# First loads in the order of need, the first Q and K by four blocks of x, and products of zeros in the first gaps

## The chip, the core and the metric

The kernel runs on one core of one Trainium2 chip. The metric is the device time of one execution in microseconds, and lower is better. The program is recorded in full before it runs: a planner written in Python inside the kernel decides the order of every instruction on every engine, and the chip then executes that fixed order, each engine in sequence, held back only by semaphores.

## The reference

Two attention layers with 32 heads of 32 columns over 2048 positions of 1024 columns each. Both share the shape of the projections; only the set of keys differs.

```python
qkv = (x @ wqkv).reshape(B, S, 3, H, Dh)            # q, k, v
# A: each position sees itself and 7 positions at steps of 2 behind it
# B: each position sees the 256 positions up to itself
scores = einsum("bhqd,bhkd->bhqk", q, k) * Dh ** -0.5
scores = where(mask, scores, -1e9)
o = einsum("bhqk,bhkd->bhqd", softmax(scores), v)
out = o.transpose(0, 2, 1, 3).reshape(B, S, D) @ wo
# result: concatenate([A, B], axis=-1)
```

## The kernel before, in words

The work is cut into eight units of 512 positions. Units 0 to 3 are layer B (called dense), units 4 to 7 are layer A (windows). A unit has eight groups of four heads. For each group the kernel computes Q and K (128 columns of heads by 512 positions), the scores, the softmax, and the product with V; after the groups comes the product with wo.

Precision comes from splitting. Each float32 operand becomes a high part in fp32r and a low part, the difference. A product of two operands is three matmuls, in the order of `TERMS`: high by high, high by low, low by high, each 128x128 by 128x512. `parts` (L222) makes the split: a cast on ACT (L228) or on DVE (L231) gives the high part, a subtraction on DVE (L234) gives the low part. One contraction block of Q therefore needs three matmuls, and Q and K of one group need 2 x 8 x 3 = 48.

`Stream` is the list of weights and x blocks in the order of use. The first six items are x block pair 0, the weights of Q, x pair 1, the weights of K, x pair 2 and x pair 3; each is 128 rows of 1024 floats (512 KB). An x item holds two contraction blocks; a weight item holds all eight, four in each half. `load_to` (L161) issues the first loads on the ACT queue: items 0 and 1 as halves in turn, then items 2 to 5 whole. Item 2 goes into the third raw buffer, items 3 to 5 borrow the room of `pbuf`, which is not needed yet. Later loads go on the POOL queue, each when a raw buffer is free again. `split_to` (L187) records the splits: at first items 0 and 1 half by half, then the others as the products reach them.

The product items of all units stand in the list `gemm`; three more lists hold the two rounds of score products (`ones`, `twos`) and the small product `rows` (`aux`). The loop at the end takes, at each step, the item that the planner's `Clock` says can start first. In the first group the order of the products is written by hand (the line with `x[0] + q[:2] + x[1] ...`). Ahead of it stand ten products of zeros (`WARM`), which read the still unused tile `qst[1]` after a memset.

In a dense group the first round (`first`, matmul `s<-kst,qst`) gives scores whose row maximum and sum DVE and ACT take. `log_sum` then turns both into one number per row, kept as a high and a low part in `hl`. The matmul `s<-ident,hl` (`rows`) turns these numbers over, DVE spreads them into the lower rows of `qst`, and only then can the second round (`s<-qst,kst`) run. The planner lets `rows` start at `e2 + HL_LATE`, which is 0.8 us after it believes `hl` is done. All four kinds of score product share a ring of four PSUM banks, `rs`.

Of the kernel before, what the change touches and what calls it, by code (L numbers as in the profile page):

```python
# [7 lines left out]
F32 = mybir.dt.float32  # L8
F32R = mybir.dt.float32r
# [5 lines left out]
P = 128  # L15
NG = 8
NK = 8
S = 512
# [3 lines left out]
NRAW, NP, NO, NS = 3, 768, 10, 4  # L22
# [7 lines left out]
CHUNK, ASKED, LEFT, FETCHED = 256, 150, 290, 7.0  # L30
EXTRA, EACH = 246, 5.2
P_LATE = 1.5
HL_LATE = 0.8
VPARTS = ((0,4),(4,2),(6,2))
V_SLOTS = {0:0,5:1,7:2}
O_SLOTS = {2: (0, 1), 3: (2, 3), 4: (4, 5), 5: (6, 7)}
# [14 lines left out]
C1, C3, CG, CV = 0.108, 0.2, 0.231, 0.242  # L51
CW = 1.36
ORDER = (0, 1, 2, 3, 4, 5, 6, 7)
BANK_LATE = 0.0
EARLY, WARM = 1.0, 10
TERMS = ((0, 0), (0, 1), (1, 0))


class Clock:
# [6 lines left out]
    HOLD = dict(sp=0.63, act=0.35, pool=0.6)  # L66
    MOVE = dict(load=(2.12, 0.14), store=(0.64, 0.4), copy=(1.18, 0.56),
                halo_out=(0.4, 0.68), halo_in=(0.55, 0.6), halo_few=(0.28, 0.51),
                half=(1.0, 0.14), part=(0.33, 0.56))

    def __init__(self):
        self.free = dict(pe=0.0, act=0.0, dve=0.0, pool=0.0, sp=0.0)
# [73 lines left out]
class Stream:  # L146
# [13 lines left out]

    def load_to(self, n):  # L161
        while not self.loaded:
            self.raw = {i: (self.raws.tile([P, 1024], F32, tag="raw", name="raw"), []) for i in range(2)}
            for h in range(2):
                for i in range(2):
                    raw, t = self.raw[i]
                    ap = self.items[i][1]
                    self.nc.scalar.dma_start(raw[:, S * h:S * h + S], ap[:, h] if len(ap.shape) == 3 else ap[:, S * h:S * h + S])
                    t.append(self.ck.load("half", self.ck.now))
            self.loaded = 2  # L170
        self.wanted = max(self.wanted, n)
        while self.loaded < min(n, len(self.items)):
            gate = self.gates.get(self.loaded)
            if gate and not gate():
                return
            k = self.loaded - NRAW
            if self.loaded >= self.wide and (self.loaded - self.wide) % (2 * NRAW) < NRAW:
                raw = self.room()
            else:
                raw = self.more[k] if 0 <= k < len(self.more) else self.raws.tile([P, 1024], F32, tag="raw", name="raw")  # L180
            ap = self.items[self.loaded][1]
            early = k < len(self.more)
            (self.nc.scalar if early else self.nc.gpsimd).dma_start(raw if len(ap.shape) == 2 else raw.rearrange("p (a b) -> p a b", a=2), ap)  # L183
            self.raw[self.loaded] = raw, (self.ck.load if early else self.ck.fetch)("load", self.ck.now)
            self.loaded += 1

    def split_to(self, n):  # L187
        while not self.split:
            (rx, tx), (rw, tw) = self.raw.pop(0), self.raw.pop(1)
            self.tiles[0], self.ready[0], self.ready[1] = [], [], []  # L190
            w = self.tiles[1] = self.wpool.tile([P, 2, 1024], F32R, tag="w", name="w")
            for h in range(2):
                c = slice(h * S, h * S + S)
                self.tiles[0].append(self.xpool.tile([P, 2, S], F32R, tag="x", name="x"))
                self.ready[0].append(self.parts(self.tiles[0][h], rx[:, c], tx[h], True))
                self.ready[1].append(self.parts(w[:, :, c], rw[:, c], tw[h], True))
            self.split = 2
            for i in range(2):
                self.ck.defer(self.ready[i][1], lambda n=i + len(self.more) + NRAW + 1: self.load_to(n))
# [44 lines left out]
def kernel(ctx, tc, xs, wqk, wv, wo, outs, units):  # L244


    nc = tc.nc
# [20 lines left out]
    ck = Clock()  # L268
# [236 lines left out]
    def latest(*ts):  # L505
        return None if any(t is None for t in ts) else max(ts)
# [788 lines left out]
    def attention(u, s):  # L1295
# [43 lines left out]
        def log_sum():  # L1339
            ln = small.tile([P, 16], F32, tag="ln", name="ln")  # L1340
            nc.scalar.activation(ln, h["sm"], AF.Ln)
            e = ck.use("act", 0.13, ck.now) - 0.03

            def parts():
                nl = small.tile([P, 16], F32, tag="nl", name="nl")
                nc.vector.tensor_tensor(nl, h["nm"], ln, op=ALU.subtract)
                hl = small.tile([P, 2, 16], F32R, tag="hl", name="hl")
                nc.vector.tensor_copy(hl[:, 0, :], nl)
                nc.vector.tensor_tensor(hl[:, 1, :], nl, hl[:, 0, :].bitcast(F32), op=ALU.subtract)
                e2 = ck.use("dve", 0.52, e, port=True)  # L1350
                aux.append(Item(lambda: latest(rs.when(BANK_LATE), e2 + HL_LATE), lambda: rows(hl), 0.08))

            ck.defer(e, parts)

        def rows(hl):
            ps, bank = rs.take()
            mm(ps[0:32, 0:P], hl.rearrange("p a b -> p (a b)"), cst["ident"], start=True, stop=True)

            def spread():

                h["rows"] = []
                for j in range(4):
                    nc.vector.tensor_tensor(q[96:P, j, :].rearrange("p (b s) -> p b s", s=P),  # L1363
                                            ps[0:32, None, 0:P].to_broadcast([32, 4, P]),
                                            cst["pick"][0:32, 4 * j:4 * j + 4, None].to_broadcast([32, 4, P]), op=ALU.mult)
# [104 lines left out]
        return one, two  # L1470


    aux, ones, twos, gemm = [], [], [], []
    for u in range(U):
        for s in range(NG):
# [4 lines left out]
    for p in plan:  # L1480
        if p[0] == "qk":
            new = qk_items(p[1], p[2])
            if p == ("qk", 0, 0):
                q, k, x = new[:NK], new[NK:], x_items(0)
                new = x[0] + q[:2] + x[1] + q[2:4] + k[:2] + x[2] + q[4:6] + k[2:4] + x[3] + q[6:] + k[4:]
            if NG - 1 not in V_SLOTS and p[2] == NG - 1 and p[1] + 1 < U:
                for g, x in reversed(list(enumerate(x_items(p[1] + 1)))):
                    new[NK + 2 * g:NK + 2 * g] = x
            gemm += new
        elif p[0] == "v":  # L1490
            new = v_items(p[1], p[2])
            if V_SLOTS.get(NG - 1) == p[2] and p[1] + 1 < U:
                m = 2 * VPARTS[p[2]][1]
                for g, x in reversed(list(enumerate(x_items(p[1] + 1)))):
                    new[m * g + XAT:m * g + XAT] = x
            gemm += new
        elif p[0] == "o":
            gemm += o_items(p[1], p[2])
        elif p[0] == "p":
            gemm += product(p[1], p[2])  # L1500
        elif p[0] == "vp":
            new = value_product(p[2])
            if VP_AT.get((p[1], NG - 1)) == p[2:] and p[1] + 1 < U:
# [6 lines left out]
    if WARM:  # L1510
        idle = qst[1][:, 0, :]
        nc.vector.memset(idle.bitcast(F32), 0.0)
        ps, bank = rs.take()
        for i in range(WARM):
            mm(ps, idle[:, :P], idle, start=True, stop=True)
        ck.free["pe"] = 0.6 + 0.43 * WARM
        rs.give(bank, ck.now)
    pos = {"a": 0, "1": 0, "2": 0, "g": 0}
    seqs = {"a": aux, "2": twos, "1": ones, "g": gemm}
    while True:  # L1520
# [21 lines left out]
        t, name = best  # L1542
# [52 lines left out]
```

## Time and profile before

| what | us |
|---|---|
| median of 3 runs (1808.05, 1811.09, 1811.22) | 1811.09 |
| the profiled execution, its own time | 1810.36 |
| the profiled execution, span from first to last instruction | 1808.5 |
| TensorE (PE) busy within the span | 1779.4 |
| VectorE (DVE) busy | 1294.4 |
| ScalarE (ACT) busy | 935.2 |
| GpSimd (POOL) busy | 417.7 |

A group of instructions in the profile is named by line, engine, operation and "written<-read" tiles. Times in a timeline row are start and length; the brackets give the idle time of the engine just before and what ended it. All matmuls are recorded through one helper, L276, so they are told apart by tiles: `g<-x,w` is a product of Q, K or of wo, `s<-qst` alone (without `kst`) is a product of zeros. ACTq, POOLq and SPq are the issuing of DMAs on those engines.

### The profile page before, as it was taken

Reading aid. Unit: us, or ns where it says so; the run is one execution under the profiler, and the core shown is the slowest. Engines: PE = TensorE matmul, PEld = TensorE weight load, DVE = VectorE, ACT = ScalarE, POOL = GpSimd, SP = SyncE. Lnnn points to the kernel's source line nnn. Section 1 sums busy time; section 2 is a strip of 40 time slices with the busy share of each in tenths; the row PEclk is TensorE's granted clock in tenths of the full one; section 3 lists DMA queues with packets and bytes.
Section 4 is the critical chain, followed back from the end, with each engine's and each line's share of the span. In section 5 each row is a group of like instructions: output and inputs, shape, how many; then the busy total and the mean of one; then the engine's idle time right before and its main releaser. Section 6 shows DMA issues by size and latency. Waiting matters only on the chain. (4 is left out here: it accounts for less than half of the span.)

```text
span 1808.5 us, 38436 instructions
## 1 busy us (share of the span) xinstructions
PE 1779.4 (98%) x14490; PEld 1439.0 (80%) x14490; DVE 1294.4 (72%) x2879; ACT 935.2 (52%) x2319; POOL 417.7 (23%) x967
## 2 busy tenths in 40 slices
PE   9999999999999999999999999999999999999999
PEld 7787778888777888777788788878887777887887
DVE  6777877768767668866678476665666768678866
ACT  5566466555666565655654543434443435356442
POOL 2323322232333233232324400110011101001220
PEclk9999999999999999999999999999999999999999
DMA  8455665645655556555556266666576568858984
GB/s 241 120 146 126 183 165 146 163 141 140 184 140 150 159 135 165 152 146 141 142 133 182 63 207 180 203 207 192 172 214 200 180 191 275 259 178 283 333 291 148
DMA packets 154649, 324.57 MB, mean 179 GB/s; under 512 B 18016, under 2 KB 58976, under 8 KB 154464
## 3 DMA queue, kind: packets, MB, share of 16 engines
q0 software_dynamic: 45792, 166.74, 30.5%
q1 hardware_dynamic: 97728, 134.40, 26.5%
q10 hardware_dynamic: 10944, 20.98, 3.1%
q8 instruction: 115, 1.88, 0.4%
q14 instruction: 70, 0.57, 0.1%
HBM read 201.33 MB, written 53.48 MB: 141 GB/s over the span
## 5 line engine op out<-in xcount | busy, mean ns | idle before, releaser
L276 PE MATMUL g<-x,w 128*128 128x512 f32 x3744 | 928.5, 395 | 5.1 <-ACT x L228 2.0
L276 PEld LDWEIGHTS g<-x,w 128*128 128x128 f32 x3744 | 692.0, 189 | 145.2 <-issue 5.6
L234 DVE TENSOR_TENSOR w<-raw,w 128x512 fp32r<-128x512 f32 x510 | 334.6, 697 | 51.7 <-ACT w L228 45.6
L276 PE MATMUL g<-w,x 128*128 128x256 f32 (+1 forms) x1872 | 332.8, 327 | 0.9 <-DVE w L234 0.7
L1323 DVE CUSTOM_DVE_ANT_0 s<-s,mask_d 128x384 f32<-128x384 f32 (+2 forms) x512 | 262.1, 553 | 98.1 <-PE s L276 96.8
L1328 ACT ACTIVATE s<-s,nm 128x384 f32<-128x384 f32 (+2 forms) x512 | 274.8, 538 | 101.4 <-DVE nm L1323 99.3
L276 PEld LDWEIGHTS g<-w,x 128*128 128x128 f32 x1872 | 276.7, 190 | 28.1 <-DVE w L234 2.2
L1387 POOL TENSOR_SCALAR_AFFINE_SELECT pbuf<-pbuf 128x128 f32<-128x128 f32 (+1 forms) x619 | 226.0, 393 | 300.9 <-ACT pbuf L1408 299.5
L1408 ACT ACTIVATE pbuf<-s 128x384 f32<-128x384 f32 (+2 forms) x480 | 202.7, 505 | 88.6 <-PE s L276 87.1
L276 PE MATMUL g<-r,w 128*128 128x512 f32 x768 | 190.8, 394 | 1.5 <-DVE r L1287 0.8
L276 PEld LDWEIGHTS g<-r,w 128*128 128x128 f32 x768 | 141.9, 188 | 30.9 <-DVE r L1287 1.8
L183 POOL DMA_DIRECT2D raw<-wqk x126 | 68.0, 540 | 417.2 <-DVE w L234 267.4
L276 PEld LDWEIGHTS s<-qst,kst 128*128 128x128 f32 x704 | 112.2, 189 | 43.6 <-ACT s L1328 17.7
L276 PE MATMUL s<-kst,qst 96*128 96x384 f32 (+2 forms) x512 | 142.9, 343 | 3.7 <-ACT s L1328 1.1
L231 DVE CAST w<-raw 128x1024 fp32r<-128x1024 f32 x176 | 122.1, 694 | 27.2 <-PE g L276 26.8
L276 PE MATMUL s<-qst,kst 128*128 128x256 f32 (+2 forms) x704 | 136.6, 302 | 4.6 <-ACT s L1328 3.5
L228 ACT CAST w<-raw 128x1024 fp32r<-128x1024 f32 (+1 forms) x80 | 82.7, 1038 | 75.8 <-PE g L276 29.0
L276 PEld LDWEIGHTS s<-kst,qst 96*128 96x128 f32 x512 | 92.9, 189 | 29.4 <-issue 6.1
L1328 ACT ACTIVATION_READ_ACCUMULATOR s<-s,nm 128x1 f32 x512 | 105.9, 207 | 0.0
L1190 ACT COPY wide<-band 32x512 f32<-32x512 f32 x128 | 79.0, 617 | 46.4 <-DVE band L1181 44.6
L276 PE MATMUL o<-pbuf,vbuf 128*32 128x384 f32 (+2 forms) x1408 | 91.1, 389 | 0.0
L1363 DVE TENSOR_TENSOR qst<-s,pick 32x512 fp32r<-32x512 f32 x128 | 79.3, 676 | 12.8 <-PE s L276 12.0
(90 smaller groups left out, 1327.7 us busy)
## 6 DMA issues: line engine op xcount, KB each, us to landing
raw<-wqk POOLq DMA_DIRECT2D x126, 512.0 KB, 4.6
raw<-wv POOLq DMA_DIRECT2D x60, 512.0 KB, 5.2
qst<-nat SPq DMA_DIRECT2D x96, 256.0 KB, 4.2
kst<-nat SPq DMA_DIRECT2D x96, 256.0 KB, 5.6
raw<-wo POOLq DMA_DIRECT2D x44, 512.0 KB, 4.9
raw<-xs POOLq DMA_DIRECT2D x28, 512.0 KB, 4.9
outs<-ost ACTq DMA_DIRECT2D x38, 256.0 KB, 2.8
kst<-halo SPq DMA_DIRECT2D x72, 128.0 KB, 4.5
```

Of the source, the lines that this page charges most:

```text
L183: (self.nc.scalar if early else self.nc.gpsimd).dma_start(raw if len(ap.shape) == 2 else raw.rearrange("p (a b) -> p a b", a=2), ap)
L228: nc.scalar.copy(t[:, 0, :], raw)
L231: nc.vector.tensor_copy(t[:, 0, :], raw)
L234: nc.vector.tensor_tensor(t[:, 1, c:c + 512], raw[:, c:c + 512], t[:, 0, c:c + 512].bitcast(F32), op=ALU.subtract)
L276: nc.tensor.matmul(out, left, right, **k)
L1190: nc.scalar.copy(diag[r:r + 32, :, :, c:c + 32], turned[r:r + 32, :, :, 1, :])
L1323: nc.vector.tensor_tensor_reduce(ps[:, :n], ps[:, :n], mask[:, cut:full], scale=-1.0, scalar=BIG, op0=ALU.add, op1=ALU.min, accum_out=nm)
L1328: nc.scalar.activation(ps[:, :n], ps[:, :n], AF.Exp, bias=nm, scale=-1.0, accum_out=sm)
L1363: nc.vector.tensor_tensor(q[96:P, j, :].rearrange("p (b s) -> p b s", s=P), ps[0:32, None, 0:P].to_broadcast([32, 4, P]), cst["pick"][0:32 ...
L1387: nc.gpsimd.affine_select(w, w, pattern=[[0, m], [step, n]], compare_op=ALU.is_ge, fill=0.0, base=base, channel_multiplier=chan)
L1408: nc.scalar.activation(w, ps[:, :pack * n].rearrange("p (j n) -> p j n", j=pack), AF.Exp)
```

## The change

The constant `HL_LATE` is gone, so the planner lets `rows` start at `e2`. The model's cost of a half load goes from 1.0 to 0.8, and a new kind `first` costs 1.4. The first loads follow the table `FIRST` of (item, half): both halves of x pair 0 and the first half of Q's weights, then x pair 1 whole, the first half of K's weights, the second half of Q's, x pair 2, the second half of K's, x pair 3. All six items are loaded and split at once, in that order. Of the first group's products, Q's first four blocks come first, then K's first four; the rest goes by two blocks of Q and two of K for each of x pairs 2 and 3. Behind Q's blocks 0, 1, 2 and 3 stand 1, 9, 1 and 4 products of zeros (`FILL`), written to the bank of the ten that were there.

```diff
-HL_LATE = 0.8
+FIRST = ((0, 0), (1, 0), (0, 1), (2, None), (3, 0), (1, 1), (4, None), (3, 1), (5, None))
+FILL = ((1, 1), (2, 9), (3, 1), (4, 4))
...
-                half=(1.0, 0.14), part=(0.33, 0.56))
+                half=(0.8, 0.14), first=(1.4, 0.14), part=(0.33, 0.56))
...
+            for i, h in FIRST:
+                raw, t = self.raw[i]
+                ap = self.items[i][1]
+                if h is None:
+                    self.nc.scalar.dma_start(raw.rearrange("p (a b) -> p a b", a=2), ap)
+                    t[:] = [self.ck.load("first", self.ck.now)] * 2
+                else:
                     self.nc.scalar.dma_start(raw[:, S * h:S * h + S], ap[:, h] if len(ap.shape) == 3 else ap[:, S * h:S * h + S])
-                    t.append(self.ck.load("half", self.ck.now))
-            self.loaded = 2
+                    t[h] = self.ck.load("half", self.ck.now)
+            self.loaded = 6
...
+            for i, g in FIRST:
+                raw, t0 = self.raw[i]
+                for h in (0, 1) if g is None else (g,):
+                    c = slice(h * S, h * S + S)
+                    t = self.tiles[i][:, :, c] if self.items[i][0] == "w" else self.tiles[i][h]
+                    self.ready[i][h] = self.parts(t, raw[:, c], t0[h], True)
+            self.split = 6
...
-                aux.append(Item(lambda: latest(rs.when(BANK_LATE), e2 + HL_LATE), lambda: rows(hl), 0.08))
+                aux.append(Item(lambda: latest(rs.when(BANK_LATE), e2), lambda: rows(hl), 0.08))
...
+    idle = qst[1][:, 0, :]
+
+    def fill(at, n):
+
+        def run():
+            mm(ps, idle[:, :P], idle, start=True, stop=True)
+
+        def after(last):
+            if last:
+                rs.give(bank, ck.now + ck.SEM)
+
+        return [(lambda: 0.0, run, CG, lambda i=i: after(at == FILL[-1][0] and i == n - 1)) for i in range(n)]
...
-                new = x[0] + q[:2] + x[1] + q[2:4] + k[:2] + x[2] + q[4:6] + k[2:4] + x[3] + q[6:] + k[4:]
+                f = dict(FILL)
+                new = x[0] + sum([q[i:i + 1] + fill(i + 1, f.get(i + 1, 0)) for i in range(4)], [])
+                for i in (1, 2, 3):
+                    new[new.index(q[2 * i]) if i < 2 else len(new):0] = x[i]
+                    if i == 1:
+                        new += k[:4]
+                    else:
+                        new += q[2 * i:2 * i + 2] + k[2 * i:2 * i + 2]
```

The first place where the order moves is the start. On PE (`s<-qst` are products of zeros, `g<-x,w` those of Q and K) before, and then in the change:

```order
L276 MATMUL s<-qst_123 128x512 x10
L276 MATMUL g<-x,w 128x512 x90
L276 MATMUL s<-kst_124,qst_122 128x128 x4
L276 MATMUL g<-x,w 128x512 x6
L276 MATMUL s<-kst_124,qst_122 128x256 x2
```

```order
L288 MATMUL s<-qst_124 128x512 x10
L288 MATMUL g<-x,w 128x512 x3
L288 MATMUL s<-qst_124 128x512
L288 MATMUL g<-x,w 128x512 x3
L288 MATMUL s<-qst_124 128x512 x9
L288 MATMUL g<-x,w 128x512 x3
L288 MATMUL s<-qst_124 128x512
L288 MATMUL g<-x,w 128x512 x3
L288 MATMUL s<-qst_124 128x512 x4
L288 MATMUL g<-x,w 128x512 x84
```

Fifteen products of zeros now stand among the first twelve real ones, and the 84 that follow run on without another kind between them. On ACT, at the same place, the loads and the first casts (`pbuf` is the borrowed room) before, and then in the change:

```order
L168 DMA raw<-xs 128x512
L168 DMA raw<-wqk 128x512
L168 DMA raw<-xs 128x512
L168 DMA raw<-wqk 128x512
L183 DMA raw<-xs 128x1024
L183 DMA pbuf<-wqk 128x1024
L183 DMA pbuf<-xs 128x1024 x2
L228 CAST x<-raw 128x512
L228 CAST w<-raw 128x512
L228 CAST x<-raw 128x512
L228 CAST w<-raw 128x512
```

```order
L175 DMA raw<-xs 128x512
L175 DMA raw<-wqk 128x512
L175 DMA raw<-xs 128x512
L172 DMA raw<-xs 128x1024
L175 DMA pbuf<-wqk 128x512
L175 DMA raw<-wqk 128x512
L172 DMA pbuf<-xs 128x1024
L175 DMA pbuf<-wqk 128x512
L172 DMA pbuf<-xs 128x1024
L240 CAST w<-raw 128x512
L240 CAST x<-raw 128x512 x3
L240 CAST w<-pbuf 128x512
```

There is one load more, x pair 1 moves from the fifth place to the fourth, and the second half of Q's weights from the fourth to the sixth. The first cast of x has gone to DVE.

The second place is on PE, ahead of the `rows` product of the sixth group. Here before, and then in the change:

```order
L276 MATMUL s<-kst_125,qst_123 128x384
L276 MATMUL g<-x,w 128x512 x3
L276 MATMUL s<-kst_125,qst_123 128x384 x4
L276 MATMUL o<-pbuf,vbuf_127 32x384 x8
L276 MATMUL s<-qst_122,kst_124 128x256 x4
L276 MATMUL s<-qst_122,kst_124 128x128 x4
L276 MATMUL s<-kst_125,qst_123 128x384 x3
L276 MATMUL o<-pbuf,vbuf_127 32x256 x4
L276 MATMUL o<-pbuf,vbuf_127 32x128 x4
L276 MATMUL g<-x,w 128x512 x3
L276 MATMUL s<-ident,hl 32x128
```

```order
L288 MATMUL s<-kst_126,qst_124 128x384 x2
L288 MATMUL g<-x,w 128x512 x3
L288 MATMUL s<-kst_126,qst_124 128x384 x3
L288 MATMUL o<-pbuf,vbuf_128 32x384 x8
L288 MATMUL s<-qst_123,kst_125 128x256 x4
L288 MATMUL s<-qst_123,kst_125 128x128 x4
L288 MATMUL s<-kst_126,qst_124 128x384 x3
L288 MATMUL o<-pbuf,vbuf_128 32x256 x4
L288 MATMUL o<-pbuf,vbuf_128 32x128 x4
L288 MATMUL s<-ident,hl 32x128
```

The three `g` products that stood between the last first-round product and `rows` now stand behind it. The third place is the same one of the twenty-third group, before and then in the change:

```order
L276 MATMUL o<-pbuf,vbuf_127 32x128 x4
L276 MATMUL s<-kst_124,qst_122 128x384
L276 MATMUL g<-x,w 128x512 x6
L276 MATMUL s<-kst_124,qst_122 128x384
L276 MATMUL g<-x,w 128x512 x6
L276 MATMUL s<-ident,hl 32x128
```

```order
L288 MATMUL o<-pbuf,vbuf_128 32x384 x4
L288 MATMUL o<-pbuf,vbuf_128 32x256 x4
L288 MATMUL o<-pbuf,vbuf_128 32x128 x4
L288 MATMUL s<-kst_125,qst_123 128x384
L288 MATMUL g<-x,w 128x512 x12
L288 MATMUL s<-ident,hl 32x128
```

Here twelve `g` products stand ahead of `rows` where six stood. Between these places the choice among the lists differs in most dense groups and in part of the windows; the last tenth of the PE order is the same in both.

More of the change, by code (lines that the diff above doesn't have):

```diff
@@ L162, in load_to @@
         while not self.loaded:
[L163 to L167, printed above, removed]
+            for i in range(3):
+                self.raw[i] = self.raws.tile([P, 1024], F32, tag="raw", name="raw"), [None, None]
+            for i, raw in enumerate(self.more):
+                self.raw[3 + i] = raw, [None, None]
+            for i, h in FIRST:
[5 more added lines that the diff above has]
+                else:
                     self.nc.scalar.dma_start(raw[:, S * h:S * h + S], ap[:, h] if len(ap.shape) == 3 else ap[:, S * h:S * h + S])
-                    t.append(self.ck.load("half", self.ck.now))
-            self.loaded = 2
+                    t[h] = self.ck.load("half", self.ck.now)
+            self.loaded = 6
         self.wanted = max(self.wanted, n)
@@ L188, in split_to @@
         while not self.split:
[L189 to L199, printed above, removed]
+            for i in range(6):
+                self.ready[i] = [None, None]
+                if self.items[i][0] == "w":
+                    self.tiles[i] = self.wpool.tile([P, 2, 1024], F32R, tag="w", name="w")
+                else:
+                    self.tiles[i] = [self.xpool.tile([P, 2, S], F32R, tag="x", name="x") for h in range(2)]
+            for i, g in FIRST:
[5 more added lines that the diff above has]
+            self.split = 6
+            for i in range(6):
+                del self.raw[i]
+                self.ck.defer(max(self.ready[i]), lambda n=min(i, 2) + len(self.more) + NRAW + 1: self.load_to(n))
         while self.split < min(n, len(self.items)):
@@ L1484 @@
                 q, k, x = new[:NK], new[NK:], x_items(0)
-                new = x[0] + q[:2] + x[1] + q[2:4] + k[:2] + x[2] + q[4:6] + k[2:4] + x[3] + q[6:] + k[4:]
+                f = dict(FILL)
[4 more added lines that the diff above has]
+                        new += k[:4]
+                    else:
+                        new += q[2 * i:2 * i + 2] + k[2 * i:2 * i + 2]
             if NG - 1 not in V_SLOTS and p[2] == NG - 1 and p[1] + 1 < U:
@@ L1509 @@
     ck.defer(0.0, constants)
[L1510 to L1517, printed above, removed]
+    nc.vector.memset(idle.bitcast(F32), 0.0)
+    ps, bank = rs.take()
+    for i in range(WARM):
+        mm(ps, idle[:, :P], idle, start=True, stop=True)
+    ck.free["pe"] = 0.6 + 0.43 * WARM
     pos = {"a": 0, "1": 0, "2": 0, "g": 0}
```

## The prediction

> **What bounds the kernel now.** I read the page first, then busy time by stretches of PE, then the timeline of the first 24 us, then the waits of PE.
>
> ```profile
> PE 1779.4 (98%) x14490; PEld 1439.0 (80%) x14490; DVE 1294.4 (72%) x2879; ACT 935.2 (52%) x2319; POOL 417.7 (23%) x967
> ```
>
> PE is busy for 98% of 1808.5 us, so time is to be had in two places only: in the 29.1 us where PE has nothing, and where it works slowly. The stretches show both (columns: stretch, its length, busy time and matmuls, granted clock, DMA share, GB/s).
>
> ```profile
> core 0: us, PE busy (x), PEclk, DMA share, GB/s
> 6.40:9.80 3.40, 1.94 (x6) 1.00 0.93 310
> 9.90:16.60 6.70, 5.96 (x13) 0.50 0.91 352
> 10.60:23.20 12.60, 12.56 (x42) 0.76 0.47 180
> 23.20:150.00 126.80, 126.56 (x728) 1.00 0.57 155
> 150.00:220.00 70.00, 64.62 (x385) 1.00 0.66 168
> ```
>
> Between 9.9 and 16.6 us the clock is granted at half; from 23.2 to 150 us PE is practically full. The timeline of PE shows what stands ahead of the slow stretch.
>
> ```profile
> 1.53 4.63 PE L276 MATMUL s<-qst 128*128 128x512 f32 x10 [1.53 <-DVE qst L1512]
> 5.98 0.90 PE L276 MATMUL g<-x,w 128*128 128x512 f32 x2
> 7.14 1.50 PE L276 MATMUL g<-x,w 128*128 128x512 f32 x4 [0.27 <-DVE w L234]
> 10.64 1.95 PE L276 MATMUL g<-x,w 128*128 128x512 f32 x3 [2.00 <-ACT x L228]
> 16.86 6.55 PE L276 MATMUL g<-x,w 128*128 128x512 f32 x28
> ```
>
> A row's length holds the last product's own 0.39 us, so 28 products at full clock take (6.55 - 0.39) / 27 = 0.228 us each. From 10.64 to the end of the first group's K at 23.2 stand 42 products; at full clock they are worth 42 x 0.228 = 9.6 us, and they took 12.6. The half clock costs 3.0 us there. The six products before, worth 1.4 us, are spread over 5.98 to 8.64, and then PE idles for 2.00 us until x pair 1 has been cast.
>
> **The start, step by step.** What PE waits for are loads and splits.
>
> ```profile
> 4.79 0.62 ACT L228 CAST x<-raw 128x512 fp32r<-128x512 f32 x1 [2.70 <-DMA raw<-xs]
> 5.31 0.61 ACT L228 CAST w<-raw 128x512 fp32r<-128x512 f32 x1
> 8.10 0.62 ACT L228 CAST w<-raw 128x512 fp32r<-128x512 f32 x1 [1.65 <-DMA raw<-wqk]
> 9.97 1.14 ACT L228 CAST x<-raw 128x512 fp32r<-128x512 f32 x2 [1.25 <-DMA raw<-xs]
> 11.23 1.04 ACT L228 CAST w<-pbuf 128x1024 fp32r<-128x1024 f32 x1
> 12.51 2.41 ACT L228 CAST x<-pbuf 128x512 fp32r<-128x512 f32 x4 [0.23 <-DMA pbuf<-xs]
> 3.67 1.08 ACTq L183 DMA_DIRECT2D pbuf<-xs  x2
> ```
>
> The four halves (1 MB) were in by 8.10, x pair 1 (1.5 MB) by 9.97, and each further 512 KB 1.3 us later. In the new order x pair 1 is complete after 1.25 MB, between those two: I take 9.0, bounds 8.1 and 9.97. The ninth load costs ACT one more issue of 0.5 us (1.08 for two), so ACT is free near 5.2 instead of 4.79; the first x cast has moved to DVE, the first w cast starts at 5.2 to 5.3 as before, and the first product stays near 5.9. The subtractions are next.
>
> ```profile
> 6.25 0.84 DVE L234 TENSOR_TENSOR w<-raw,w 128x512 fp32r<-128x512 f32 x1
> 7.01 0.84 DVE L234 TENSOR_TENSOR x<-raw,x 128x512 fp32r<-128x512 f32 x1
> 10.62 1.29 DVE L234 TENSOR_TENSOR x<-raw,x 128x512 fp32r<-128x512 f32 x2 [1.18 <-ACT x L228]
> 13.52 2.49 DVE L234 TENSOR_TENSOR x<-pbuf,x 128x512 fp32r<-128x512 f32 x4
> 23.45 0.60 ACT L568 ACTIVATE nat<-g 128x512 fp32r<-128x512 f32 x1 [2.12 <-PE g L276]
> ```
>
> The low part of w is ready at 5.85 + 0.84 = 6.7, the low part of x's second block at 7.5. So Q's block 0 ends at 6.95, one product of zeros at 7.2, Q's block 1 at 8.0, and the nine of zeros at 8.0 + 9 x 0.228 = 10.05. By then x pair 1 has its first cast (9.0 + 0.6); its first low part is ready at 10.35, which costs a stall of 0.1. From 10.05 stand Q's blocks 2 and 3, K's first four and the eight of x pairs 2 and 3: 14 blocks or 42 products, and five of zeros, together 47 x 0.228 = 10.7. K ends at 20.9 instead of 23.2: **2.3 us saved**. The ten products of zeros before x pair 1 lie in time in which PE would wait anyway; the five after it are on the path and cost 1.1, already in the sum. Later stalls I cost at nothing, and what hides them is this. x pair 3 is still the end of the same 3 MB, so it is split near 16.0 as before (13.52 + 2.49) and first needed at 10.05 + 35 x 0.228 = 18.0; the cover is 2 us. The weights of the second group come over POOL; its second load now waits until Q's weights are split near 12.4 (their second half is loaded later), and a V load stands behind it. In the page such loads land 4.6 us after issue,
>
> ```profile
> raw<-wqk POOLq DMA_DIRECT2D x126, 512.0 KB, 4.6
> PE s L276 <- ACT s L1328: 4.6, 7, 1.1
> PE s L276 <- DVE hl L1349: 3.7, 3, 1.5
> PE s L276 <- DVE qst L1363: 1.3, 3, 0.5
> ```
>
> that is near 17.6, and K of the second group begins at 20.9 + 24 x 0.228 = 26.4, 2 us of splits ahead of it; without that cover each microsecond of lateness would be one of time. The bounds of the start: 2.7 saved if x pair 1 is in by 8.1 and no low part is late; 1.5 if it comes at 9.97 (its low part then ends near 11.2, which puts block 2 behind by 0.8).
>
> Whether the clock stays up decides 3.0 us more. The ten products of zeros came before the clock was full at 6.4, so zeros count as work. With PE then busy 57% of 6.4 to 9.8 (1.94 of 3.40) it fell at 9.9, and with the products of zeros in the same stretch only the waits for low parts remain, about 0.5 of 3.4 us. I take it as staying full. The Trainium skill (TensorE: Matmul & The Clock Gate, section Why this matters for your kernels) asks for no PE-idle gap over about 3 us between bursts; the trace disagrees, since a gap of 2.00 us was enough here, and by that rule the clock would not have fallen before and nothing but the idle time could be saved. The same page of the skill (section Part 1: The HAM clock gate) says that the deciding window of 3.4 us runs freely, whenever the kernel starts; the trace agrees in that the half clock lasts 6.7 us, two such windows.
>
> **The delay taken from `rows`.** 29 of the 32 `rows` products do not wait today; the three that do cost 3.7 us. The order shows where this changes.
>
> ```profile
> 175.57 0.43 PE L276 MATMUL s<-kst,qst 96*128 96x384 f32 x1
> 179.25 0.22 PE L276 MATMUL s<-ident,hl 128*32 128x128 f32 x1 [1.46 <-DVE hl L1349]
> 216.49 0.22 PE L276 MATMUL s<-ident,hl 128*32 128x128 f32 x1 [1.05 <-DVE hl L1349]
> 721.31 1.55 PE L276 MATMUL g<-x,w 128*128 128x512 f32 x6
> 724.04 0.22 PE L276 MATMUL s<-ident,hl 128*32 128x128 f32 x1 [1.17 <-DVE hl L1349]
> ```
>
> From the last first-round product to `rows` the chain took 179.25 - 175.57 = 3.7 us in the sixth group. There the three `g` products that covered part of it are gone: 0.7 us lost. In the twenty-third, six more stand ahead: 6 x 0.228 covers the 1.17, which is gained. In the seventh only six `g` products (1.4 us) remain behind the last first-round product; 3.7 less these and the product itself leaves a wait near 2.0 against 1.05, 0.9 lost. What waits behind `rows` on PE is the next `g` work, and no queue of DMAs. The sum is a loss of 0.4; for the earlier second round on the other side, and for the changed order of the bank ring, I find no row that gives a sign. From nearest rows the bounds are the three waits of `s` above, 9.6 us together: a third less or a third more, 3.2 either way. I take +0.6 in all, near the counted 0.4. PE's own work is otherwise the same, except the 15 products of zeros, which are in the start's sum.
>
> **The sum.** 1808.5 - 2.3 + 0.6 = 1806.8 us of span; with the 1.86 around it (1810.36 - 1808.5) 1808.7 for an execution like the profiled one, which stands 0.73 below the median of the runs. Against the median 1811.09 it makes **1809.4 us**, a gain of 0.09%. About 0.2%, 3.6 us, is what a measurement of this kernel can tell from no change.
>
> **Rivals.** *The later order pays.* `rows` come earlier, second rounds spread out, and a third of the 9.6 us of score waits goes: 1811.09 - 2.3 - 3.2 = 1805.6. For it speaks that the twenty-third group loses its wait; against it that the sixth and seventh gain some.
>
> *The later order costs more than the start gives: slower.* The place is the dense part from 150 us on, already the thinnest stretch (5.4 of 70 us idle). With `rows` taken at once, a wait at `hl` holds everything behind it on PE, and the four banks then turn over in a bunch, so that products wait for the exponentials too. At two thirds more on the score waits, 9.6 x 0.67 = 6.4: 1811.09 - 2.3 + 6.4 = 1815.2. It decides from 2.3 us of added waits on. For it speak the sixth and seventh groups; against it the 29 groups with no wait.
>
> *The gaps are not filled in time.* x pair 1 comes at 9.97 and PE falls idle long enough for the clock to halve again over half of the old 6.7 us: the gain of 1.5 is met by a loss of 3.35 / 2 = 1.7 and the +0.6: 1811.09 - 1.5 + 1.7 + 0.6 = 1811.9. The change would then not do what it says. Against it speak the ten products of zeros that did hold the clock.
>
> *The gate's phase.* One run of the three, 1808.05, lies 3.0 us below the two others, as much as the half clock costs, so executions may differ in when the clock is granted; the median is then one with the drop, like the profiled one. In the change the filled gaps leave nothing to drop, but the rise could come later than 6.4 us by half of the 6.7 us stretch. All that runs in those 3.35 us at half speed then costs up to 1.7: 1809.4 + 1.7 = 1811.1. For it speaks the spread of the runs, against it that nothing in this one trace shows another moment of the rise. The skill's free-running window is a rule that would give this.
>
> **Chances.** Forecast 0.46, with its own range 1806.5 to 1812; the later order pays 0.22; costs more 0.18; gaps unfilled 0.08; phase 0.06. Faster by over 0.2% is below 1807.5: nearly all of the second case and 0.16 of the first, 0.36. Slower is above 1814.7: the third and a rest, 0.22. Within: 0.42. The range 1804.5 to 1815 leaves out the outer halves of the second and third.
>
> **What would show it.** The first 24 us show the start: clock 1.00 from 6.4 on, the second evacuation of `g` (L568 before, at 23.45) near 21.1, the first x pair 1 product near 10.1. If that product comes after 11 the load estimate is wrong; if the clock shows 0.50 after 9.9 the filling is. The waits on `hl` should read near 4, with the largest in the sixth and seventh groups; a sum over 8 would mean that the delay had been needed. The last tenth of PE's order is the same, so the shift before it should arrive at the end.

## The result and the profile after

| | before | changed |
|---|---|---|
| median, us | 1810.72 (6 runs, 1808.05 to 1811.22) | 1816.20 (6 runs, 1813.98 to 1819.88) |
| ratio to before, 95% interval | 1 | 1.0034 (1.0024 to 1.0044) |
| profiled execution, its time and its span, us | 1810.36, 1808.5 | 1818.5, 1816.7 |

The changed kernel is slower by 0.34%, and the whole interval lies above 1. The time is on the side of the second rival, and outside the range.

The first 24 us ended as the prediction said. The stretches of PE after the change (stretch, length, busy time and products, granted clock, DMA share, GB/s), and the rows of PE and ACT there:

```profile
6.40:9.80 3.40, 3.40 (x15) 1.00 0.95 341
9.90:16.60 6.70, 6.70 (x32) 1.00 0.89 334
```

```profile
8.13 2.24 PE L288 MATMUL s<-qst 128*128 128x512 f32 x9
8.47 1.14 ACT L240 CAST x<-raw 128x512 fp32r<-128x512 f32 x2 [2.04 <-DMA raw<-xs]
10.21 0.84 PE L288 MATMUL g<-x,w 128*128 128x512 f32 x3
21.07 0.60 ACT L580 ACTIVATE nat<-g 128x512 fp32r<-128x512 f32 x1 [0.76 <-PE g L288]
```

The clock stays full where it had been halved, x pair 1 is used from 10.21 on (foretold 10.05), and the second evacuation starts at 21.07 instead of 23.45. In this pair of executions 2.4 us were gained, and all the loss comes later. x pair 1 itself was in by 8.47, earlier than the 9.0 that was foretold: what holds its first product until 10.21 is the nine products of zeros. The page of the changed kernel has more busy time on PE (1779.4 before), and its largest waits, with those that nothing releases (`issue`), are these:

```profile
PE 1785.2 (98%) x14505; PEld 1445.2 (80%) x14505; DVE 1306.1 (72%) x2901; ACT 928.8 (51%) x2308; POOL 411.8 (23%) x957
```

```profile
PE s L288 <- ACT s L1340: 5.8, 8, 1.2
PE s L288 <- DVE hl L1361: 4.0, 3, 2.4
PE g L288 <- ACT w L240: 3.8, 3, 2.2
PE g L288 <- issue: 1.6, 3, 0.9
PE s L288 <- issue: 1.1, 1, 1.1
```

The waits on `hl` are 4.0 us, as foretold; those on the exponentials have grown from 4.6 to 5.8, those on ACT's casts of w from 2.2 to 3.8, and those that nothing releases from 0.7 to 2.7. The last two before the change:

```profile
PE g L276 <- ACT w L228: 2.2, 3, 1.1
PE o L276 <- issue: 0.7, 1, 0.7
```

What the prediction had nothing of shows in the stretches around the longest waits, again of PE in the changed kernel:

```profile
173.80:177.20 3.40, 1.07 (x17) 1.00 1.04 241
177.20:180.60 3.40, 3.38 (x13) 0.50 1.09 221
201.10:204.50 3.40, 2.40 (x12) 1.00 0.75 200
204.50:207.90 3.40, 3.40 (x16) 0.50 0.99 240
1351.40:1354.80 3.40, 1.25 (x4) 1.00 0.18 67
1354.80:1358.20 3.40, 3.40 (x9) 0.50 0.72 195
1450.40:1453.80 3.40, 1.56 (x20) 1.00 0.66 177
1453.80:1457.20 3.40, 3.40 (x10) 0.50 0.87 278
```

After each stretch of 3.4 us in which PE worked 1.07, 1.25 or 1.56 us, the next 3.4 us ran at half clock, and 3.4 us at half speed do 1.7 us less work; at 201.1 a stretch with 2.40 us of work had the same sequel. In the profiled execution of the kernel before no stretch behind the start had it. This is one of the two emptiest there (the other, at 214.6, had 1.81):

```profile
177.00:180.40 3.40, 1.94 (x13) 1.00 1.07 214
180.40:183.80 3.40, 3.40 (x28) 1.00 1.00 228
```

With that a ledger closes. For each profiled execution the table gives the span; the start of the second group's first product, which is the 49th `g` product (*start*); the idle time of PE behind it, in the dense units and in the window units; half of PE's busy time in stretches of half clock behind it, which is what they cost; and what is left of the span.

| us | span | start | idle, dense | idle, windows | half clock later | left |
|---|---|---|---|---|---|---|
| before | 1808.5 | 23.2 | 13.6 | 8.0 | 0 | 1763.6 |
| changed | 1816.7 | 20.9 | 15.3 | 10.6 | 6.8 | 1763.2 |

The difference of 8.2 us is -2.4 at the start, +1.65 and +2.55 of idle time, +6.8 of half clock and -0.4.

The half clock of this pair is not typical. Each run's mean granted clock is on record, and one less that clock, times the span, is what half clock cost the run, start included. On the mean this is 6.1 us over the six runs of the changed kernel, and 4.4 to 4.8 over the three sets of 22 to 35 runs of the kernel before. The clock is recorded to 0.001, 1.8 us in one run, so this is rough: half clock makes about 1.5 us between the kernels, where this pair has 3.4 (6.8 later, less 3.4 at the start of the kernel before). Most of the 5.5 us between the medians is there at full clock too.

Two things were to be found out: which part of the change brings the waits, and whether they come from that part or from the planner's choices, which any edit of the planner changes.

### The profile page after: what moved, and what is told of

The parts are those of the page before. It is cut to its first block, busy times and chain, and to the rows that moved or that the text cites. A ratio compares the mean times of both kernels' runs of the same rounds, so it can differ in the third digit from the quotient of the medians.

```text
span 1816.7 us, 38479 instructions
## 1 busy us (share of the span) xinstructions
PE 1785.2 (98%) x14505; PEld 1445.2 (80%) x14505; DVE 1306.1 (72%) x2901; ACT 928.8 (51%) x2308; POOL 411.8 (23%) x957
## 4 chain that ended last, share of the span: by engine, by line
PE 86%; DVE 5%; issue 3%; DMA 3%; ACT 2%; POOL 0%; ACTq 0%; DVEq 0%; SPq 0%; POOLq 0%
PE g L288 68%; PE s L288 12%; PE o L288 6%; DMA raw<-xs 1%; DVE w L246 1%; DVE x L246 1%; DMA kst<-nat 1%; ACT s L1340 1%; DVE w L243 0%; DMA qst<-nat 0%; POOL pbuf L1399 0%; DVE s L1335 0%; ACT w L240 0%; DMA kst<-halo 0%; DVE band L1163 0%
## 5 line engine op out<-in xcount | busy, mean ns | idle before, releaser
L1399 POOL TENSOR_SCALAR_AFFINE_SELECT pbuf<-pbuf 128x128 f32<-128x128 f32 (+1 forms) x609 | 220.2, 390 | 324.6 <-ACT pbuf L1420 323.2
L288 PEld LDWEIGHTS s<-qst,kst 128*128 128x128 f32 x704 | 112.9, 189 | 38.0 <-ACT s L1340 13.6
L240 ACT CAST w<-raw 128x1024 fp32r<-128x1024 f32 (+1 forms) x76 | 78.7, 1038 | 83.7 <-PE g L288 39.4
```

Of the source, the lines that this page charges most:

```text
L240: nc.scalar.copy(t[:, 0, :], raw)
L288: nc.tensor.matmul(out, left, right, **k)
L1399: nc.gpsimd.affine_select(w, w, pattern=[[0, m], [step, n]], compare_op=ALU.is_ge, fill=0.0, base=base, channel_multiplier=chan)
```

## The experiments

**Each half of the change alone, the zeros alone, and an edit without content.** `start_only` is the changed kernel with the delay back; `delay_only` is the kernel before without it; `after_nofill` is the changed kernel without the products of zeros in the gaps; `neutral_hi` changes a cost that only the planner believes in.

```diff
 # start_only, against the changed kernel
+HL_LATE = 0.8
-aux.append(Item(lambda: latest(rs.when(BANK_LATE), e2), lambda: rows(hl), 0.08))
+aux.append(Item(lambda: latest(rs.when(BANK_LATE), e2 + HL_LATE), lambda: rows(hl), 0.08))
 # delay_only, against the kernel before
-HL_LATE = 0.8
+HL_LATE = 0.0
 # after_nofill, against the changed kernel
-FILL = ((1, 1), (2, 9), (3, 1), (4, 4))
+FILL = ()
 # neutral_hi, against the kernel before
-C1, C3, CG, CV = 0.108, 0.2, 0.231, 0.242
+C1, C3, CG, CV = 0.108, 0.2, 0.232, 0.242
```

Expected of `start_only`:

> The new start as it is, with HL_LATE = 0.8 back. All theories: the first 24 us as in the changed kernel, the second evacuation of g near 21.1 us and no half clock before it. Theory delay (the loss of 10 us behind 24 us comes from rows taken without the 0.8 us): the later part is as before, so 1810.7 - 2.4 = 1808.3. Theory order (any new order of the planner moves waits, and the order before was a lucky one): the later part is longer by anything from 0 to 10 us, 1808 to 1818, with no more waits on hl than before. Theory start (the new start itself harms what follows): 1814 to 1818, as the changed kernel.

Expected of `delay_only`:

> The kernel before with HL_LATE = 0 and nothing else. Theory delay: 1810.7 + 8 to 10, so 1818 to 1821, with waits on hl or on the exponentials grown by that. Theory order: anywhere from 1808 to 1820. Theory start: within 2 us of 1810.7.

Expected of `after_nofill`:

> The changed kernel without the 15 products of zeros in the gaps (the ten ahead stay). If the products of zeros are what holds the clock: PE busy falls under 60% of the 3.4 us ahead of 9.9, the clock halves there, 42 products from about 10.1 take up to 12.6 us and K ends near 22.5 instead of 20.9. If the earlier loads alone are enough to hold it: no half clock, and K ends at or below 20.9, since the five products of zeros on the path (1.1 us) are gone. The order behind the first group is nearly that of the changed kernel, so the rest should lie near it: 1815 to 1819.

Expected of `neutral_hi`:

> The kernel before, where only the planner's belief of a product's cost goes from 0.231 to 0.232 us. Nothing is computed or loaded differently and the start is the same; only the order is another. Theory order: the time moves by several us against 1810.7, more likely up, 1808 to 1820. Theories delay and start: it stays within 2 us of 1810.7, since neither rows nor the start has changed.

| | median, us | ratio to before (95%) |
|---|---|---|
| start_only | 1815.59 | 1.0028 (1.0017 to 1.0039) |
| delay_only | 1805.93 | 0.9972 (0.9962 to 0.9982) |
| after_nofill | 1811.68 | 1.0014 (1.0001 to 1.0027) |
| neutral_hi | 1811.84 | 1.0011 (1.0001 to 1.0021) |

The theory that the delay had been needed falls at once: without it the kernel before is faster by 0.28%. The start edit alone is slower by 0.28%. But an edit without content also costs 0.11%, with an interval that just leaves out 1. Without zeros the changed kernel is 4.5 us faster than with them, where I had expected 1815 to 1819, and the clock does not fall at the start. PE in `after_nofill`, where x pair 1 is now waited for:

```profile
5.96 2.18 PE L288 MATMUL g<-x,w 128*128 128x512 f32 x6
9.05 0.49 PE L288 MATMUL g<-x,w 128*128 128x512 f32 x1 [0.92 <-ACT x L240]
9.82 12.55 PE L288 MATMUL g<-x,w 128*128 128x512 f32 x54 [0.27 <-DVE x L246]
```

54 products in 12.55 us are at full clock, (12.55 - 0.39) / 53 = 0.229 us each. The new loads and the order by blocks kept it up without zeros in the gaps. x pair 1 is used from 9.05 on instead of 10.21, so the nine zeros ahead of it were on the path too: all fifteen together cost 20.9 - 19.3 = 1.6 us for nothing.

One place shows how an order far from the edit makes a wait. In the changed kernel PE stands still ahead of 1353.55, and ACT's rows say why. PE and ACT of the changed kernel, and then of the kernel before at the same products:

```profile
1345.68 5.63 PE L288 MATMUL g<-x,w 128*128 128x512 f32 x24
1351.34 0.60 ACT L539 ACTIVATE nat<-g 128x512 f32<-128x512 f32 x1 [4.48 <-PE g L288]
1352.46 1.03 ACT L240 CAST w<-raw 128x1024 fp32r<-128x1024 f32 x1
1353.55 2.82 PE L288 MATMUL g<-x,w 128*128 128x512 f32 x7 [2.25 <-ACT w L240]
```

```profile
1343.76 5.63 PE L276 MATMUL g<-x,w 128*128 128x512 f32 x24
1349.58 2.51 PE L276 MATMUL g<-x,w 128*128 128x512 f32 x9 [0.19 <-DVE w L231]
```

In the changed kernel the planner gave the cast of the next weights to ACT, behind an evacuation that had to wait 4.48 us for the 24 products to end. So the weights came 2.25 us after PE needed them, and the clock was halved from 1354.8 on. Before, DVE made the cast in time. `start_only` has the same wait (2.24 us), `after_nofill` does not, though it loads and splits the same things: this is the planner's choice, over 1300 us behind the start.

**The new start with the planner's choices kept.** To take the choices out, four kernels emit the new loads, splits and products of the first group as they are, while the planner accounts for that group as before the change. Behind the 48th product every engine then has the order of the kernel before (`old_order`, `HL_LATE` 0.8) or of `delay_only` (`early_order`, `HL_LATE` 0). Each is made with the 15 products of zeros (`new_start`) and without (`nofill`).

```diff
+    st.open()
+    for n, (t, k) in enumerate(blocks):
+        for i, (a, b) in enumerate(TERMS):
+            nc.tensor.matmul(opened[t], ...)
+        for i in range(f.get(n + 1, 0)):
+            nc.tensor.matmul(ps, idle[:, :P], idle, start=True, stop=True)
...
-                for i, (a, b) in enumerate(TERMS):
+                for i, (a, b) in enumerate(TERMS if hg else ()):
```

Expected of `old_order_new_start`:

> The changed start whole (loads, splits, products by blocks, 15 products of zeros), while the planner decides everything behind the first group as in the kernel before, HL_LATE 0.8: behind the 48th product all engines have the order of before. Theory order (the loss of the changed kernel is the planner's new order far behind the start): 1810.2 - 2.4 = 1807.8. Theory start (the new start harms what follows, through loads or buffers): 1813 to 1817 as in the changed kernel and in start_only.

Expected of `old_order_nofill`:

> The same without the 15 products of zeros in the gaps. Theory order: 1.6 us less than with them as long as the clock holds, since K ended at 19.3 instead of 20.9 us in the run without them: 1806.2. If the clock falls in part of the executions for want of the zeros, those are up to 3.4 / 2 = 1.7 us longer each window, and the spread over the runs grows. Theory start: 1811 to 1815.

Expected of `early_order_new_start`:

> The changed start whole, and behind it the order of the kernel before with HL_LATE = 0 (delay_only, 1805.9). Both edits of the change are then in, only the planner's choices behind the start are not those that the new start led it to. Theory order: 1805.9 - 2.4 = 1803.5, 12 us below the changed kernel. Theory start: 1810 or more.

Expected of `early_order_nofill`:

> The same without the 15 products of zeros in the gaps. Theory order: 1805.9 - 4.0 = 1801.9, if the clock holds. Theory start: 1808 or more.

| | median, us | ratio to before (95%) |
|---|---|---|
| old_order_new_start | 1817.54 | 1.0033 (1.0021 to 1.0046) |
| old_order_nofill | 1809.57 | 0.9993 (0.9985 to 1.0002) |
| early_order_new_start | 1810.23 | 1.0007 (0.9996 to 1.0017) |
| early_order_nofill | 1804.48 | 0.9970 (0.9958 to 0.9981) |

Both theories were half wrong. `early_order_new_start` has both edits of the change, all 15 zeros and the same products, and is 6 us below the changed kernel: behind the same start, the order of `delay_only` is worth those 6 us. Without the zeros the two figures are 1804.48 and 1811.68, 7 us apart. But the order of the kernel before does not save the new start: `old_order_new_start` is as slow as the changed kernel. (`st.open` makes all six items' splits in the order of `FIRST`; `blocks` lists Q's and K's blocks as the change has them.) The kept orders with zeros are 5.7 and 8.0 us above those without, where I had foretold 1.6. The 8.0 is coarse: of the five runs of `old_order_new_start` two had a mean clock of 1.000 (1812.3 and 1814.5 us), three one of 0.997 (1817.5 to 1818.4).

The start of these four is not quite that of the changed kernel. The second group begins 0.8 to 1.4 us later (22.2 and 22.3 against 20.9 with zeros, 20.1 and 20.5 against 19.3 without). Of that 0.65 us is a wait which the changed kernel has not: there DVE casts these weights from 14.87 on, in the kept order it does so only at 21.51, behind an evacuation. PE of `early_order_new_start`:

```profile
22.25 3.95 PE L310 MATMUL g<-x,w 128*128 128x512 f32 x15 [0.65 <-DVE w L264]
```

The waits of `old_order_new_start` have two rows that the kernel before has not, and PE's timeline shows one of them in the middle of 128 small score products:

```profile
PE g L310 <- issue: 2.2, 1, 2.2
PE s L310 <- issue: 2.0, 1, 2.0
```

```profile
1122.89 0.27 PE L310 MATMUL s<-pbuf 32*32 32x40 f32 x6 [1.96 <-issue]
1123.09 1.10 PE L310 MATMUL g<-w,x 128*128 128x256 f32 x7
```

No engine and no DMA releases these waits. The planner knows such waits: it counts the instructions of PE in pieces of 256 (`CHUNK`) and keeps long runs of small products away from the places where the next piece is asked for (`short`). In these kernels the 15 zeros, 30 instructions with their weight loads, were not in its count. `early_order_new_start` has such a break at the same products:

```profile
1115.20 1.25 PE L310 MATMUL s<-pbuf 32*32 32x40 f32 x120
1118.18 0.28 PE L310 MATMUL s<-pbuf 32*32 32x40 f32 x8 [1.72 <-issue]
```

A stretch of half clock follows it at 1119.6, and with that the pair of profiled executions of this order nearly comes out: of 6.1 us between the spans with and without zeros, 2.1 are the later start, 1.7 the break and 1.7 more half clock.

**Is it the zeros' work or their number?** `old_order_tiny` has the same number of zero products at the same places, with 32 columns instead of 512. Three more orders were run beside it: `delay_neutral` (no delay, cost 0.232), `start_nofill` (`start_only` without zeros) and `neutral_lo` (cost 0.230).

```diff
 # old_order_tiny, against old_order_new_start
-            nc.tensor.matmul(ps, idle[:, :P], idle, start=True, stop=True)
+            nc.tensor.matmul(ps[:, :32], idle[:, :P], idle[:, :32], start=True, stop=True)
 # delay_neutral, against delay_only
-C1, C3, CG, CV = 0.108, 0.2, 0.231, 0.242
+C1, C3, CG, CV = 0.108, 0.2, 0.232, 0.242
 # start_nofill, against start_only
-FILL = ((1, 1), (2, 9), (3, 1), (4, 4))
+FILL = ()
 # neutral_lo, against the kernel before
-C1, C3, CG, CV = 0.108, 0.2, 0.231, 0.242
+C1, C3, CG, CV = 0.108, 0.2, 0.230, 0.242
```

Expected of `old_order_tiny`:

> As old_order_new_start, but each of the 15 products of zeros has 32 columns instead of 512: the same number of PE instructions at the same places, hardly any work. Theory fetch (the 30 instructions, 15 weight loads and 15 products, move the places where PE's instructions are fetched 256 at a time, and PE then runs dry for about 2 us each near 1122 and 1252 us): these two waits with no releaser come back as in old_order_new_start, about 4 us together against 0.1 without products of zeros, and the time is 1813 to 1817. Theory work (the cost is the zeros' own time on PE and their clock): no such waits, and the time of old_order_nofill, 1809.6.

Expected of `delay_neutral`:

> The kernel before with HL_LATE = 0 and the planner's cost of a product at 0.232 instead of 0.231, so another order with the same edit. Theory delay (rows without the 0.8 us is itself what made delay_only 0.28% faster): near 1806 again, with idle time of PE in the dense part near the 8.6 us of delay_only. Theory order (that was one good order among many): 1809 to 1815, with 13 to 15 us idle there, like the other orders tried.

Expected of `start_nofill`:

> The changed start without products of zeros, HL_LATE 0.8, and the planner's own order behind it. Theory order: its idle time in the dense part is another draw, 13 to 15 us, so 1808 to 1814. If the products of zeros are the main cost of the start edit, it is 4 to 6 us below start_only (1815.6), so 1809.6 to 1811.6.

Expected of `neutral_lo`:

> The kernel before with the planner's cost of a product at 0.230 instead of 0.231: one more order with nothing else changed. Theory order: 1808 to 1816, not below the kernel before by more than 2 us.

| | median, us | ratio to before (95%) |
|---|---|---|
| old_order_tiny | 1813.54 | 1.0026 (1.0015 to 1.0037) |
| delay_neutral | 1811.67 | 1.0005 (0.9997 to 1.0014) |
| start_nofill | 1810.31 | 1.0002 (0.9993 to 1.0011) |
| neutral_lo | 1812.04 | 1.0014 (1.0005 to 1.0023) |

The waits come back with hardly any work in the zeros. The waits and PE's timeline of `old_order_tiny`:

```profile
PE s L310 <- issue: 2.3, 1, 2.3
PE g L310 <- issue: 2.2, 1, 2.2
```

```profile
1119.63 1.27 PE L310 MATMUL s<-pbuf 32*32 32x40 f32 x122
1123.22 0.27 PE L310 MATMUL s<-pbuf 32*32 32x40 f32 x6 [2.32 <-issue]
```

At the same products without zeros, in `old_order_nofill`, all 128 run through:

```profile
1118.97 1.32 PE L310 MATMUL s<-pbuf 32*32 32x40 f32 x128
1120.22 1.95 PE L310 MATMUL g<-w,x 128*128 128x256 f32 x13
```

So their number is a cause of its own: with the same order, 30 instructions more ahead of these products let PE run dry in the middle of them. It is worth 4.0 us of the 8.0 (1813.54 against 1809.57). The other 4.0 are put down to the zeros' own time, but the intervals of `old_order_tiny` and `old_order_new_start` overlap. The DMA packets speak for a wait for instructions. The page counts 115 in one queue of kind instruction:

```profile
q8 instruction: 115, 1.88, 0.4%
```

That is 16 KB each. The 14505 matmuls and 14505 weight loads of PE are 113 pieces of 256, so this looks like PE's queue, and by this estimate an instruction has 64 bytes. In `old_order_tiny` one such packet starts at 1120.89, just as the 122nd product ends, and PE goes on 2.3 us later. In `old_order_nofill` one starts at 1119.12, with most of the 128 products still to run.

The other three say that `delay_only` was mostly a good draw: the same edit with another planner cost is not told apart from the kernel before. Taking the delay out was tried four times, each time with another order: the kernel before gained 0.28%, `neutral_hi` 0.06%, while `start_only` lost 0.06% and `start_nofill` 0.12%. The zeros are steadier. Each of the four kernels with the 15 full ones is slower than the same kernel without: by 4.5 us (changed), 5.3 (`start_only`), 8.0 and 5.7 (the kept orders). Where the planner orders anew, that holds the redrawn order too.

The ledger of the profiled executions, where that of `old_order_tiny` is the slowest of its twelve runs (1821.21 us):

| us | span | start | idle, dense | idle, windows | half clock later | left |
|---|---|---|---|---|---|---|
| start_only | 1813.1 | 21.5 | 15.0 | 9.3 | 5.0 | 1762.3 |
| delay_only | 1805.6 | 23.7 | 8.6 | 7.9 | 3.4 | 1762.0 |
| after_nofill | 1809.6 | 19.3 | 14.2 | 7.5 | 6.1 | 1762.6 |
| neutral_hi | 1810.1 | 21.5 | 13.4 | 8.5 | 4.8 | 1761.9 |
| old_order_new_start | 1812.5 | 22.3 | 12.8 | 13.2 | 0 | 1764.3 |
| old_order_nofill | 1807.6 | 20.5 | 13.1 | 8.1 | 1.7 | 1764.1 |
| early_order_new_start | 1808.4 | 22.2 | 8.7 | 10.3 | 5.1 | 1762.0 |
| early_order_nofill | 1802.3 | 20.1 | 8.6 | 8.7 | 3.4 | 1761.6 |
| old_order_tiny | 1819.2 | 21.0 | 12.6 | 15.3 | 6.6 | 1763.6 |
| delay_neutral | 1810.2 | 22.3 | 13.5 | 8.5 | 6.1 | 1759.8 |
| start_nofill | 1808.5 | 19.5 | 14.2 | 7.4 | 3.4 | 1764.0 |
| neutral_lo | 1811.2 | 21.8 | 10.6 | 9.9 | 6.6 | 1762.3 |

The last column stays within 4.5 us over 14 different kernels, within 2.7 without `delay_neutral`: most of what they differ in is the start, waits of PE, and half clock. Eight of the nine orders that the planner made have 10.6 to 15.3 us of idle time in the dense part, one has 8.6, and a kept order takes its figure along (8.6, 8.7 and 8.6; 13.6, 12.8, 13.1 and 12.6).

The best kernel is `early_order_nofill`, at 0.9970 of before: the new loads and the products by blocks, no zeros in the gaps, and the order of `delay_only` behind. It beats both the kernel before and the changed one. Against `delay_only` (0.9972) the two intervals overlap, and `old_order_nofill`, the new start with the order of before, is not told apart from the kernel before (0.9985 to 1.0002). So a gain from the new start is seen in the profiled starts, but not shown in the time.

## Why the prediction was wrong

**The start.** Right for the profiled pair: 2.3 us foretold, 2.4 seen, the clock full, and the first product of x pair 1 and the second evacuation within 0.2 us. One step was right for another reason: x pair 1 came 0.5 us sooner than I took, and the zeros hid it. One sum does not come out, 12.4 + 4.6 is 17.0 and not 17.6, and nothing hangs on it. As a gain of the median it was too large. Kernels with the old start begin the second group at 23.2, 23.7, 21.5, 21.8 and 22.3 us, for the half clock lasts two stretches in some executions and one in others; their mean is 22.5, and the profiled execution of before was one of the slow starts. The changed start with zeros took 20.9 and 21.5 in the planner's own order, so 1.3 us is nearer the typical gain.

**The zeros.** I costed ten of the fifteen at nothing, as covered by a wait, and took all of them to be needed for the clock. Neither held: without them no half clock came up to 25 us in any of the four profiled executions, and the second group begins 1.6 us sooner in the pair of `after_nofill`, 2.0 in that of `start_nofill`. Taken out of the changed kernel they give back 4.5 of the 5.5 us that it lost. That they also move the places of instruction fetch, I had not thought of. In the kept orders this is shown. In the changed kernel itself the planner counts them, and what they do there beyond the 1.6 us is not shown: its waits without a releaser are 2.7 us against 0.7 before, but `after_nofill` has 2.1 of them without zeros and `start_only` none with them.

**The delay taken from `rows`.** The sum of the waits on `hl` (4.0 against 3.7) came out as counted from the order, by errors that cancel: the sixth group's grew to 2.35 (2.2 was to be expected), the seventh's to 1.38 (2.0), the twenty-third's shrank from 1.17 to 0.31 (to nothing). This was not where the time went, and the second rival had the right sign with mostly the wrong place: I had put it into the bank ring and `hl`, and of the score waits only those on the exponentials grew clearly, by 1.2 us.

**The term that failed is the +0.6 for the changed order.** It was counted at the three places that I had looked at, all waits of score products in the dense part. The profiled pair shows +4.2 us of waits, over half of them in the windows, where the prediction named no place, and +6.8 of half clock behind them, for which it had no term at all (over all runs the two kernels differ by about 1.5 in half clock, start included). I had priced a wait at its own length. A wait that empties PE for around half of a 3.4 us stretch can cost another 1.7 us. And I had argued with the delay and the loads, where the zeros and the planner's choices weigh more: the changed kernel took 1811.68 without zeros, and 1810.23 with them and the order of `delay_only`, instead of 1816.20. Two changes of a planner's cost by 0.4% moved the kernel before by +0.11% and +0.14%. Why most new orders of this planner are no better than the one it had is not shown; that the constants had been chosen with that order would be an explanation, and it was not tried.

## What to carry to other kernels

Where a planner makes the order, hold it fixed before judging an edit: otherwise the edit's own few microseconds drown in the redrawn order, and a change without content belongs beside each experiment. Price a wait of PE twice, by its length and by the half clock that can follow it. Filling a gap is not free even when the engine would idle: the filler can outlast the gap, and its instructions move every later place of instruction fetch. Before comparing two profiles, see from the clocks of all runs whether they are typical.

## What the runs showed of the hardware

The clock fell after waits far below 3 us: 2.25 us of idle time in one piece at 1353, or 1.84 us in two pieces near 1452. The Trainium skill (TensorE: Matmul & The Clock Gate, section Why this matters for your kernels) asks only that gaps stay under about 3 us; by that rule none of the later half clocks would have come, and the runs do not bear it out. What decides is not settled here: at 201.1 a stretch with 2.40 of 3.40 us busy was followed by half clock too, while in the kernel before one with 1.94 was not. In each of the 14 profiles the times at which half clock begins lie whole multiples of 3.41 us behind the first grant of full clock. Cut on that grid, 22 stretches at full clock had at most 1.59 us of work, and 21 of them were followed by half clock; above 2.91 us none was; between the two, 15 were and 234 were not.

A run of 128 small products (32x40) broke off after 122 for 2.32 us, with no engine and no DMA of the program to wait for, once 30 instructions more stood ahead of it. A 16 KB packet of the instruction queue started as it broke off.
